# Gate and value weights loaded in pairs of row blocks, half of the low words cast on ScalarE, the scale of P in its cast, phi's sum on GpSimd

## The chip, the cores and the metric

The program runs on one core of a Trainium2 chip. The time is the device time of one execution in microseconds (us). The kernel before was timed three times; the median is 652.61 us (652.18 to 654.96). The profile was taken of one further execution of 654.12 us, whose traced span is 652.4 us.

Engines are called PE (TensorE, matmul), DVE (VectorE), ACT (ScalarE), POOL (GpSimd) and SP (the queue that issues nearly all DMAs). Each engine works through its own instructions in a fixed order, which is settled when the program is built.

## The reference, cut to what matters

```python
# attention: q, k, v of shape (4, 8, 576, 64)
a = softmax(causal(q @ k.T / sqrt(64)));  local = a @ v
phi(x) = where(x > 0, x, exp(x) - 1) + 1
mem = (phi(q) @ M_prev) / (phi(q) @ z_prev + 1e-6)
out = sigmoid(beta) * mem + (1 - sigmoid(beta)) * local
# gated FFN on x = out as (2304, 512)
xn = x / rms(x) * rms_g
y = (silu(xn @ w_gate) * (xn @ w_val)) @ w_out    # 512 -> 1536 -> 512
```

The weights w_gate, w_val (512 x 1536) and w_out (1536 x 512) arrive as float64 and are turned into float32 on the chip.

## The kernel before

**Tiling.** The 2304 rows are 18 blocks of 128 (n = 0 to 17), numbered so that blocks 0 and 1, 2 and 3 and so on form nine chunks (c = 0 to 8) of 256 rows for the FFN. A block's attention has a unit per head, or for short causal lengths per group of up to four heads.

**A unit of attention** (n from 2 on) goes through `u_scores` (matmuls of kT and qT in float16 high and low parts into `sc`; L514 or L538 on DVE adds the mask, writes S and the row minimum `nm`; L521 or L552 on DVE then adds the constant LNP = 15 ln 2 to `nm`), `u_exp` (L560 on ACT: exp(nm - S), so that P comes out times 2^15; L565 on ACT: cast to float16 P), `u_lo` (L574: the low half, S - P, on DVE, or for every second unit of blocks 4 to 7 on POOL; then one DMA transpose P to PT) and `u_pv` (L598 to L600: PT times v). Blocks 0 and 1 go through float32 forms of the same steps (`scores32`, `pv32`, `evac32`), which need no transposing DMA.

**phi** (`phi_calc`): exp on ACT (L355), then two instructions on DVE: min with 1 (L356), and max with q + 1 (L357). The result is cast, transposed by DMA to phT and multiplied with M (L635).

**The FFN** of chunk 0 runs in float32 (`m_proj`, L858: `gv` from xT and `wgv`; `m_down`, L912) since its weights are not yet split into float16 parts; chunks 1 to 8 run in float16 parts (L865 and L920 to L922). L858 needs both halves of xT of chunk 0, which blocks 0 and 1 write on DVE (L707), and all eight pieces of the first third of the weights.

**The weights.** w_gate and w_val are 24 pieces of 128 x 512 float64 (512 KB), ordered by third t, then gate or value, then row block cc. `load_w` (L744) brings a piece on SP's queue into one of six slots in the tile `wo`, which is not yet used for w_out; `w_conv` calls `f64_to_f32`, which runs ACT L774 (high word to float32), DVE L775 (low word shifted right by 29) and DVE L776 (the two joined), and then issues the load that takes the slot over. w_out follows in 12 pieces of the same size by `load_wo` and `wo_conv`, through the same function.

**What sets the order.** The work list `A` (attention) and lists of FFN closures are woven by `run` and `a_until` by hand-set targets; then the scheduler of the build places each instruction on its engine by its own simulated timeline and the priorities in `PRIO`. So an edit of durations or sizes can shift instructions anywhere.

Of the kernel before, what the change touches and what calls it, by code (L numbers as in the profile page):

```python
# [25 lines left out]
HORD = "k0 q0 M0 k1 q1 v0 M1 v1 w0 w1 w2 w3 w4 w5"  # L26
LAG = 3
LAG0 = 8
NA = 2
# [4 lines left out]
C1 = 8  # L34
# [10 lines left out]
P_HI = "a"  # L45
# [3 lines left out]
RING = 6  # L49
# [8 lines left out]
def attn_memory_moe_kernel(  # L58
# [435 lines left out]
    def u_scores(n, h0):  # L494
# [25 lines left out]

        nc.vector.tensor_scalar(nm0, nm0, LNP, None, op0=ALU.add)  # L521
        Ssb[(n, h0)] = (s, w, nm0)

    def tail_scores(n, h, s, nm, t, w):
# [27 lines left out]
        nc.vector.tensor_scalar(nm0, nm0, LNP, None, op0=ALU.add)  # L552
        Ssb[(n, h)] = (s, w + P, nm0)

    def u_exp(n, h0):
        s, w, nm = Ssb[(n, h0)]
        G = group(n)
        for g in range(G):
            v_ = s[:, g * w : (g + 1) * w]
            nc.scalar.activation(v_, v_, AF.Exp, bias=nm[:, g : g + 1], scale=-1.0)  # L560
        p16 = sb.tile([P, 2 * (NI * P + P)], F16, tag="P16", name="P16")
        if P_HI[(h0 // G) % len(P_HI)] == "d" and n < 4:
            nc.vector.tensor_copy(p16[:, : G * w], s[:, : G * w])
# [167 lines left out]
    NR = RING  # L731
    PRE = {"p": nc.gpsimd, "s": nc.sync, "a": nc.scalar}[PREQ]

    def hold(p, at):

        assert not any(abs(at - x) < 2 for x in held.values())
        held[p] = at
        return wo[:, at : at + 2, :].rearrange("p a f -> p (a f)")

    def load_w(m, cc, t):  # L740
        w = (w_gate, w_val)[m]
        p = piece(m, cc, t)
# [23 lines left out]
    def f64_to_f32(raw, dst, p):  # L766
# [5 lines left out]
        r = raw.rearrange("p (f w) -> p f w", w=2)  # L772
        ri, di = r.bitcast(I32), dst.bitcast(I32)
        nc.scalar.activation(dst, r[:, :, 1], AF.Prelu, scale=2.0 ** -112, alpha=2.0 ** 32)  # L774
        nc.vector.tensor_scalar(ri[:, :, 0], ri[:, :, 0], 29, None, op0=ALU.logical_shift_right)  # L775
        nc.vector.scalar_tensor_tensor(  # L776
            out=di, in0=di, scalar=3, in1=ri[:, :, 0], op0=ALU.logical_shift_left, op1=ALU.bitwise_or
# [252 lines left out]
    with tc.high_priority(HP) if HP else contextlib.nullcontext():  # L1030
# [3 lines left out]
            "M": load_M, "w": lambda p: load_w(*pcs[p]),  # L1034
# [150 lines left out]
    def conv(t):  # L1185
        return [lambda i=i: w_conv(i) for i, x in enumerate(pcs) if x[2] == t]
# [101 lines left out]
```

## Time and profile before

| what | value |
|---|---|
| three runs, median | 652.61 us |
| profiled execution | 654.12 us |
| its span | 652.4 us |
| outside the span | 1.7 us |
| PE busy | 607.4 us, 93% |
| DVE busy | 470.6 us, 72% |
| ACT busy | 384.5 us, 59% |
| POOL busy | 172.6 us, 26% |
| first float32 projection (L858) starts | 50.83 us |
| first down projection of chunk 0 (L912) starts | 124.24 us |

Busy time of PE is the union of matmuls whose ends are modelled, so a busy PE need not be at its peak. The profile's shares are means over stages: the first 50 us (loads, blocks 0 and 1), the stretch to about 145 us (chunk 0 of the FFN in float32, conversion of the weights, blocks 2 and 3), the stretch to about 240 us (weights split into float16 parts, blocks 4 to 7), and the rest, in which PE works almost without a gap. Idle time of an engine counts only where what it waits for is late.

### The profile page before, as it was taken

How to read it: one execution, taken by the hardware profiler on the slowest of the kernel's cores; microseconds unless marked ns; L12 is line 12 of the kernel's file. 1: busy time of each engine (PE TensorE's matmuls, PEld its weight loads, DVE VectorE, ACT ScalarE, POOL GpSimd, SP SyncE). 2: the span in 40 equal slices, each digit the busy share in tenths (PEclk: the TensorE clock that was granted, in tenths of full speed). 3: DMA queues.
4: the chain of work that ended last, by engine and by line, in shares of the span. 5: the costliest groups of instructions: out<-in, count | busy, mean ns of one | idle time of the engine just before them, and what ended most of it. 6: DMA issues, size and time to landing. Idle time of an engine off the chain costs nothing.

```text
span 652.4 us, 16021 instructions
## 1 busy us (share of the span) xinstructions
PE 607.4 (93%) x6131; PEld 473.9 (73%) x6131; DVE 470.6 (72%) x1444; ACT 384.5 (59%) x803; POOL 172.6 (26%) x257
## 2 busy tenths in 40 slices
PE   6789998797998789998999999999999999999996
PEld 4767787546866468787777787777878788888774
DVE  4787997877999666796877857967877757862221
ACT  3654675567689756575667666856665555442222
POOL 5020221210473333231242312522232212112211
PEclk8588998998999889999999999999999999999999
DMA  7995899529547897546759863595656464440001
GB/s 259 406 354 175 238 292 197 98 25 224 86 96 156 162 182 143 89 90 138 155 116 178 142 117 74 99 165 103 130 120 114 90 87 86 84 77 17 33 1 33
DMA packets 188524, 88.63 MB, mean 136 GB/s; under 512 B 173568, under 2 KB 173600, under 8 KB 188448
## 3 DMA queue, kind: packets, MB, share of 16 engines
q1 hardware_dynamic: 187680, 85.49, 60.3%
q0 software_dynamic: 768, 2.12, 1.0%
q8 instruction: 48, 0.79, 0.5%
q14 instruction: 28, 0.23, 0.1%
HBM read 36.20 MB, written 4.72 MB: 63 GB/s over the span
## 4 chain that ended last, share of the span: by engine, by line
PE 60%; DMA 14%; DVE 13%; ACT 7%; issue 3%; SPq 1%; POOL 0%; ACTq 0%; POOLq 0%; DVEq 0%
PE gv L865 29%; PE out L921 5%; PE out L920 5%; PE out L922 5%; PE out L912 3%; PE sc L508 3%; DMA phT<-row 3%; DMA PT<-P 2%; DMA wo<-in_moe_w_val_dram 2%; PE gv L858 2%; PE sc L534 2%; DMA kT<-row 2%; DVE S L514 2%; DVE P L574 2%; DMA kv<-in_qkv_dram 1%
## 5 line engine op out<-in xcount | busy, mean ns | idle before, releaser
L865 PE MATMUL gv<-xT,wgv 128*128 128x256 f16 x2304 | 313.9, 275 | 3.1 <-DMA xT<-x 3.1
L865 PEld LDWEIGHTS <-wgv 128*128 128x128 f16 x2304 | 221.9, 98 | 39.3 <-issue 4.2
L891 POOL TENSOR_TENSOR h<-th,h 128x256 f16<-128x256 f32 x96 | 73.1, 761 | 267.9 <-ACT h L890 210.0
L560 ACT ACTIVATE S<-S,nm 128x256 f32<-128x256 f32 (+4 forms) x128 | 75.5, 611 | 55.6 <-DVE nm L521 41.1
L508 PE MATMUL sc<-kT,qT 128*128 128x128 f16 x608 | 84.6, 222 | 3.5 <-DVE nm L514 1.5
L574 DVE TENSOR_TENSOR P<-S,P 128x512 f16<-128x512 f32 (+2 forms) x84 | 62.8, 748 | 34.4 <-ACT P L565 34.1
L876 DVE SCALAR_TENSOR_TENSOR th<-th,gv 128x256 f32<-128x256 f32 x96 | 39.9, 415 | 56.4 <-ACT th L875 55.9
L875 ACT ACTIVATE th<-gv,wt 128x256 f32<-128x256 f32 x96 | 44.9, 468 | 52.6 <-PE gv L865 51.6
L921 PE MATMUL out<-wo,h 128*128 128x512 f16 x192 | 72.8, 379 | 0.0
L920 PE MATMUL out<-wo,h 128*128 128x512 f16 x192 | 71.8, 379 | 0.0
L922 PE MATMUL out<-wo,h 128*128 128x512 f16 x192 | 71.6, 379 | 0.0
L514 DVE CUSTOM_DVE_ANT_0 S<-sc,mask,qsc 128x256 f32<-128x256 f32 (+3 forms) x112 | 62.1, 573 | 7.4 <-PE sc L508 5.5
L565 ACT CAST P<-S 128x512 f16<-128x512 f32 (+2 forms) x100 | 59.7, 597 | 10.0 <-DMA PT<-P 8.9
L890 ACT CAST h<-th 128x256 f16<-128x256 f32 x96 | 38.6, 402 | 43.8 <-DVE th L879 43.1
L598 PE MATMUL loc<-v,PT 128*128 128x65 f16 x304 | 50.6, 195 | 13.0 <-DMA PT<-P 12.8
L508 PEld LDWEIGHTS <-qT 128*128 128x128 f16 x608 | 51.4, 99 | 9.9 <-issue 3.1
L600 PE MATMUL loc<-v,PT 128*128 128x65 f16 x304 | 50.4, 195 | 0.0
L599 PE MATMUL loc<-v,PT 128*128 128x64 f16 x304 | 50.3, 195 | 0.0
L879 DVE SCALAR_TENSOR_TENSOR th<-th,wt,gv 128x256 f32<-128x256 f32 x96 | 45.8, 477 | 1.7
L858 PE MATMUL gv<-xT,wgv 128*128 128x256 f32 x192 | 46.8, 397 | 0.1
L598 PEld LDWEIGHTS <-PT 128*128 128x128 f16 x304 | 29.5, 98 | 19.4 <-DMA PT<-P 16.6
L858 PEld LDWEIGHTS gv<-xT,wgv 128*128 128x128 f32 x192 | 36.9, 198 | 6.2 <-issue 0.9
(226 smaller groups left out, 1112.9 us busy)
## 6 DMA issues: line engine op xcount, KB each, us to landing
kv<-in_qkv_dram SPq DMA_DIRECT2D x16, 512.0 KB, 4.5
wo<-in_moe_w_gate_dram SPq DMA_DIRECT2D x12, 512.0 KB, 7.8
wo<-in_moe_w_val_dram SPq DMA_DIRECT2D x12, 512.0 KB, 6.5
q<-in_qkv_dram SPq DMA_DIRECT2D x18, 256.0 KB, 3.1
wo<-in_moe_w_out_dram SPq DMA_DIRECT2D x8, 512.0 KB, 4.3
qT<-qT SPq DMA_DIRECT2D x32, 128.0 KB, 2.6
out_dram<-res SPq DMA_DIRECT2D x16, 256.0 KB, 2.4
pre<-in_qkv_dram POOLq DMA_DIRECT2D x8, 256.0 KB, 7.3
```

The costliest lines, as they stand in the source:

```text
L508: nc.tensor.matmul(t[:, g * w + j * P : g * w + (j + 1) * P], qT[n][:, t2, h, :], kT[blk_of[(b, j)]][:, h, :], start=(t2 == 0), stop=(t2 = ...
L514: nc.vector.tensor_tensor_reduce(out=s[:, g * w : (g + 1) * w], in0=t[:, g * w : (g + 1) * w], in1=mask[:, m0 : m0 + w], scale=qsc[n][:, 5:6],
L560: nc.scalar.activation(v_, v_, AF.Exp, bias=nm[:, g : g + 1], scale=-1.0)
L565: nc.scalar.copy(p16[:, : G * w], s[:, : G * w])
L574: eng.tensor_tensor(p16[:, w : 2 * w], s[:, :w], p16[:, :w], ALU.subtract)
L598: nc.tensor.matmul(a, phi_, vhi, start=(j == 0), stop=False)
L858: nc.tensor.matmul(o, wgv[:, 1 + p, o0 : o0 + P], xT[0][:, cc, :], start=(cc == 0), stop=(cc == NC - 1))
L865: nc.tensor.matmul(o, lhs, xT[c][:, rhs, :], start=(cnt == 0), stop=(cnt == 3 * NC - 1))
L891: nc.gpsimd.tensor_tensor(h16[:, 1], th, h16[:, 0], ALU.subtract)
L920: nc.tensor.matmul(o, hh, whi, start=(f == 0), stop=False)
L921: nc.tensor.matmul(o, hh, wlo, start=False, stop=False)
L922: nc.tensor.matmul(o, hl, whi, start=False, stop=(f == NF - 1))
```

## The change

Four edits.

1. `load_w(k)` brings two row blocks (1 MB) in one DMA into a slot of twice the size; three slots instead of six. There are 12 such loads instead of 24, and `w_conv(k)` converts 128 x 1024 at a time.
2. In `f64_to_f32` the low word of every second call (odd k of the pairs, odd f of w_out) is shifted by an ACT activation (Copy with a scale and a bias that truncates, written as an integer) instead of DVE's shift.
3. LNP is no longer added to `nm`, except in the units whose low half is on POOL. Instead the casts of P carry the factor 2^15: `hi_cast` (ACT, with a constant scale) and `lo_cast` (DVE scalar_tensor_tensor, S times the constant minus P).
4. For n >= 2 phi's q + 1 is computed in place on POOL (tensor_scalar), and one DVE instruction does min and max.

```diff
-HORD = "k0 q0 M0 k1 q1 v0 M1 v1 w0 w1 w2 w3 w4 w5"
+HORD = "k0 q0 M0 k1 q1 v0 M1 v1 w0 w1 w2"
-RING = 6
+RING = 3
         nc.scalar.activation(ph, qst[n], AF.Exp)
-        nc.vector.tensor_scalar(ph, ph, 1.0, None, op0=ALU.min)
-        nc.vector.scalar_tensor_tensor(
-            out=ph, in0=qst[n], scalar=1.0, in1=ph, op0=ALU.add, op1=ALU.max
-        )
+        if n < NA:
...
+        else:
+            nc.gpsimd.tensor_scalar(qst[n], qst[n], 1.0, None, op0=ALU.add)
+            nc.vector.scalar_tensor_tensor(
+                out=ph, in0=ph, scalar=1.0, in1=qst[n], op0=ALU.min, op1=ALU.max
+            )
@@ u_scores (tail_scores drops the line altogether)
-        nc.vector.tensor_scalar(nm0, nm0, LNP, None, op0=ALU.add)
+        if lo_on_pool(n, h0):
+            nc.vector.tensor_scalar(nm0, nm0, LNP, None, op0=ALU.add)
@@ u_exp, u_lo
-            nc.scalar.copy(p16[:, : G * w], s[:, : G * w])
+            hi_cast(p16[:, : G * w], s[:, : G * w], PSCALE)
-        eng = nc.gpsimd if lo_on_pool(n, h0) else nc.vector
-        eng.tensor_tensor(p16[:, w : 2 * w], s[:, :w], p16[:, :w], ALU.subtract)
+        if lo_on_pool(n, h0):
+            nc.gpsimd.tensor_tensor(p16[:, w : 2 * w], s[:, :w], p16[:, :w], ALU.subtract)
+        else:
+            lo_cast(p16[:, w : 2 * w], s[:, :w], PSCALE, p16[:, :w])
@@ load_w
-        raws[p] = hold(p, 2 * (p % NR))
+        m, cc, t = pcs[2 * k]
+        raws[k] = hold(k, 4 * (k % RING), 2)
         nc.sync.dma_start(
-            out=raws[p].bitcast(I64), in_=w[cc * P : (cc + 1) * P, t * 512 : (t + 1) * 512]
+            out=raws[k].bitcast(I64),
+            in_=(w_gate, w_val)[m][cc * P : (cc + 2) * P, t * 512 : (t + 1) * 512].rearrange(
+                "(a p) f -> p a f", a=2
+            ),
         )
@@ f64_to_f32
-        nc.vector.tensor_scalar(ri[:, :, 0], ri[:, :, 0], 29, None, op0=ALU.logical_shift_right)
+        if p % 2:
+            nc.scalar.activation(
+                top, low, AF.Copy, bias=-0.5 + 15.0 * 2.0 ** -21, scale=2.0 ** -29 - 2.0 ** -49
+            )
+        else:
+            nc.vector.tensor_scalar(top, words(raw.bitcast(I32))[..., 0], 29, None, op0=ALU.logical_shift_right)
@@ w_conv
-        f64_to_f32(raws.pop(p), wgv[:, 1 + p, :], i)
+        f64_to_f32(raws.pop(k), wgv[:, 1 + p : 3 + p, :], k)
```

The built order shifts with it. On DVE, where the scores of block 0 begin, the kernel before has the first weight piece (L775 and L776) between block 0's copies (L375) and the scores' masking (L429), interleaved with block 1's phi:

```order
L375 COPY q_0_148<-tp 128x512
L775 TENSOR_SCALAR wo<-wo 128x512
L356 TENSOR_SCALAR ph<-ph 128x512
L776 SCALAR_TENSOR_TENSOR wgv<-wgv,wo 128x512
L357 SCALAR_TENSOR_TENSOR ph<-q_120,ph 128x512
L429 ISA S,nm_163<-sc,mask 128x128
```

At the same place on DVE the changed kernel has (its lines L379, L355, L356 and L433 are the former L375, L356, L357 and L429):

```order
L379 COPY q_0_145<-tp 128x512
L355 TENSOR_SCALAR ph<-ph 128x512
L356 SCALAR_TENSOR_TENSOR ph<-q_120,ph 128x512
L433 ISA S,nm_160<-sc,mask 128x128
L433 ISA nm_160 128x1
```

No weight stands ahead of block 0's scores any more; the first conversion follows behind them. Down to the second write of xT (L707 before) DVE has 14 shifts and 13 joins of 128 x 512 before, and 3 shifts and 5 joins of 128 x 1024 now, beside one shift of w_out in both.

On DVE, in the units of block 2 (about 102 us in the trace of before), two heads are masked (L514, `nm` is the row minimum), and LNP's addition (L521) stands behind the low half of another unit, a join and an FFN step:

```order
L514 ISA nm 128x1
L574 TENSOR_TENSOR P_840<-S,P_840 128x512
L776 SCALAR_TENSOR_TENSOR wo<-wo,rawo_1550 128x512
L876 SCALAR_TENSOR_TENSOR h32v<-h32v,gv_1273 128x256
L521 TENSOR_SCALAR nm<-nm 128x2
L514 ISA S,nm<-sc,mask,qsc 128x256
```

In the changed kernel, on DVE at that place (L518 is the former L514, L792 the former L776):

```order
L895 SCALAR_TENSOR_TENSOR h32v<-h32v,gv_1217 128x256
L518 ISA S,nm<-sc,mask,qsc 128x256
L518 ISA nm 128x1
L518 ISA S,nm<-sc,mask,qsc 128x256
L518 ISA nm 128x1
L792 SCALAR_TENSOR_TENSOR wo<-wo,rawo_1453 128x512
```

`nm` is complete with the masking itself, and no instruction stands between it and ACT's exp.

On PE, the last float32 projection of chunk 0 (L858, gate and value of the last 128 columns) stands in the kernel before behind the first 24 products of PT and v of block 2, between scores and sums of squares of the weights (L146):

```order
L508 LDWEIGHTS qT_817
L508 MATMUL sc<-kT_857,qT_817 128x128
L858 MATMUL gv_1339<-xT_307,wgv 128x256 x8
L146 LDWEIGHTS wo
L146 MATMUL csum<-wo 128x128
```

In the changed kernel, on PE, it is complete (L874 is the former L858) ahead of the first such product (L603, the former L598):

```order
L874 MATMUL gv_1283<-xT_304,wgv 128x256 x5
L512 LDWEIGHTS qT_777
L512 MATMUL sc<-kT_726,qT_777 128x128
L874 MATMUL gv_1283<-xT_304,wgv 128x256 x3
L603 LDWEIGHTS PT
L603 MATMUL loc_0_859<-v_0_562,PT 128x65
```

The projections have moved ahead of the attention of blocks 2 and 3. From chunk 1 on the two orders of PE keep within a few units of each other.

## Rows read from the trace of the kernel before

**Rows 1.** The page, busy time (us), share of the span and instructions of each engine.

```profile
PE 607.4 (93%) x6131; PEld 473.9 (73%) x6131; DVE 470.6 (72%) x1444; ACT 384.5 (59%) x803; POOL 172.6 (26%) x257
```

**Rows 2.** Busy time by stretch, instructions in brackets; granted clock as share of full.

```profile
core 0: us, PE busy (x) PEld busy (x) DVE busy (x) ACT busy (x) POOL busy (x), PEclk, DMA share, GB/s
...
60.00:80.00 20.00, 19.94 (x127) 16.00 (x125) 18.88 (x66) 12.30 (x23) 4.79 (x5) 1.00 0.63 179
...
100.00:120.00 20.00, 15.18 (x161) 12.99 (x159) 15.35 (x54) 10.60 (x23) 3.63 (x4) 0.91 0.77 157
...
220.00:240.00 20.00, 13.64 (x172) 11.29 (x172) 13.73 (x43) 13.27 (x27) 5.72 (x8) 0.74 1.03 207
460.00:500.00 40.00, 40.00 (x426) 31.43 (x425) 31.09 (x97) 26.01 (x56) 10.85 (x16) 1.00 0.66 125
```

**Rows 3.** Who PE waited for over the span: us in total, times, longest.

```profile
PE loc L598 <- DMA PT<-P: 12.8, 13, 2.3
...
PE mem L635 <- DMA phT<-row: 4.0, 3, 3.3
PE gv L865 <- DMA xT<-x: 3.1, 1, 3.1
```

**Rows 4.** PE's timeline: first projection, first down projection (start, us, instruction, count).

```profile
50.83 6.41 PE L858 MATMUL gv<-xT,wgv 128*128 128x256 f32 x22
...
124.24 7.11 PE L912 MATMUL out<-wo,h32e 128*128 128x512 f32 x16
```

**Rows 5.** DVE's timeline at the start; in brackets the idle time before and its releaser.

```profile
13.43 0.43 DVE L775 TENSOR_SCALAR wo<-wo 128x512 int32<-128x512 int32 x1 [2.13 <-DMA wo<-in_moe_w_gate_dram]
...
15.37 0.28 DVE L429 CUSTOM_DVE_ANT_0 S<-sc,mask 128x128 f32<-128x128 f32 x1
...
17.40 0.69 DVE L375 COPY k<-tp 128x512 f32<-128x512 f32 x1
...
30.46 0.43 DVE L775 TENSOR_SCALAR wo<-wo 128x512 int32<-128x512 int32 x1 [1.06 <-DMA wo<-in_moe_w_val_dram]
```

**Rows 6.** Groups by line and shape: count, busy us, mean ns of one, idle before.

```profile
L774 ACT ACTIVATE wgv<-wo 128x512 f32<-128x512 f32 x24 | 15.3, 673 | 5.8 <-DMA wo<-in_moe_w_val_dram 3.0 <-DMA wo<-in_moe_w_gate_dram 2.8
...
L775 DVE TENSOR_SCALAR wo<-wo 128x512 int32<-128x512 int32 x32 | 13.5, 421 | 4.8 <-DMA wo<-in_moe_w_val_dram 2.2 <-DMA wo<-in_moe_w_gate_dram 2.1 <-DMA wo<-in_moe_w_out_dram 0.4
...
L776 DVE SCALAR_TENSOR_TENSOR wgv<-wgv,wo 128x512 int32<-128x512 int32 x24 | 16.4, 684 | 2.1 <-ACT wgv L774 1.6
...
L574 DVE TENSOR_TENSOR P<-S,P 128x384 f16<-128x384 f32 x24 | 15.3, 638 | 5.9 <-ACT P L565 5.9
...
L574 DVE TENSOR_TENSOR P<-S,P 128x640 f16<-128x640 f32 x16 | 14.3, 895 | 3.9 <-ACT P L565 3.8
...
L565 ACT CAST P<-S 128x512 f16<-128x512 f32 x52 | 31.9, 614 | 6.8 <-DMA PT<-P 6.3
...
L521 DVE TENSOR_SCALAR nm<-nm 128x1 f32<-128x1 f32 x64 | 9.5, 148 | 0.8
...
L356 DVE TENSOR_SCALAR ph<-ph 128x512 f32<-128x512 f32 x18 | 8.7, 484 | 6.4 <-ACT ph L355 5.8 <-POOL v L116 0.5
```

**Rows 7.** ACT's waits for `nm` from 50 to 250 us, then one unit's timeline.

```profile
ACT S L560 <- DVE nm L521: 10.4, 10, 3.2
...
112.41 0.09 DVE L514 DVE_READ_ACCUMULATOR2_ANT nm<- 128x1 f32 x1
...
114.01 0.17 DVE L521 TENSOR_SCALAR nm<-nm 128x2 f32<-128x2 f32 x1
...
114.22 0.92 ACT L560 ACTIVATE S<-S,nm 128x256 f32<-128x256 f32 x2 [2.65 <-DVE nm L521]
```

**Rows 8.** POOL's two shapes of 128 x 512, and one low half on DVE beside POOL's work.

```profile
L229 POOL COPY Mz<-M 128x512 f32<-128x512 f32 x2 | 1.2, 610 | 6.4 <-DMA M<-in_M_prev_dram 6.4
...
L116 POOL TENSOR_TENSOR v<-kv,v 128x512 f16<-128x512 f32 x18 | 22.6, 1269 | 41.2 <-ACT v L113 41.2
...
185.33 1.51 DVE L574 TENSOR_TENSOR P<-S,P 128x384 f16<-128x384 f32 x1
```

More of the change, by code (lines that the diff above doesn't have):

```diff
@@ L33 @@
 T32 = "dadda"
-C1 = 8
 C2 = 8
@@ L551, in tail_scores @@
         nm0 = nm[:, 1:2]
-        nc.vector.tensor_scalar(nm0, nm0, LNP, None, op0=ALU.add)
         Ssb[(n, h)] = (s, w + P, nm0)
@@ L561, in u_exp @@
         p16 = sb.tile([P, 2 * (NI * P + P)], F16, tag="P16", name="P16")
-        if P_HI[(h0 // G) % len(P_HI)] == "d" and n < 4:
-            nc.vector.tensor_copy(p16[:, : G * w], s[:, : G * w])
+        if lo_on_pool(n, h0):
+            nc.scalar.copy(p16[:, : G * w], s[:, : G * w])
         else:
-            nc.scalar.copy(p16[:, : G * w], s[:, : G * w])
+            hi_cast(p16[:, : G * w], s[:, : G * w], PSCALE)
         Ssb[(n, h0)] = (s, G * w, p16)
@@ L730, in attn_memory_moe_kernel, with hold, load_w @@
     raws = {}
-    NR = RING
     PRE = {"p": nc.gpsimd, "s": nc.sync, "a": nc.scalar}[PREQ]
[L734 to L742, printed above, removed]
-        raws[p] = hold(p, 2 * (p % NR))
+    def hold(p, at, n=1):
+        assert not any(at < y and x < at + 2 * n for x, y in held.values())
+        held[p] = (at, at + 2 * n)
+        r = wo[:, at : at + 2 * n, :].rearrange("p (a b) f -> p a (b f)", a=n)
+        return r if n > 1 else r[:, 0]
+    def load_w(k):
+        m, cc, t = pcs[2 * k]
+        raws[k] = hold(k, 4 * (k % RING), 2)
         nc.sync.dma_start(
-            out=raws[p].bitcast(I64), in_=w[cc * P : (cc + 1) * P, t * 512 : (t + 1) * 512]
+            out=raws[k].bitcast(I64),
+            in_=(w_gate, w_val)[m][cc * P : (cc + 2) * P, t * 512 : (t + 1) * 512].rearrange(
+                "(a p) f -> p a f", a=2
+            ),
         )
@@ L766, in f64_to_f32, with words @@
     def f64_to_f32(raw, dst, p):
-        r = raw.rearrange("p (f w) -> p f w", w=2)
-        ri, di = r.bitcast(I32), dst.bitcast(I32)
-        nc.scalar.activation(dst, r[:, :, 1], AF.Prelu, scale=2.0 ** -112, alpha=2.0 ** 32)
-        nc.vector.tensor_scalar(ri[:, :, 0], ri[:, :, 0], 29, None, op0=ALU.logical_shift_right)
+        def words(x):
+            return x.rearrange("p a (f w) -> p a f w" if len(x.shape) == 3 else "p (f w) -> p f w", w=2)
+        high, low = words(raw)[..., 1], words(raw.bitcast(U32))[..., 0]
+        top, di = words(raw.bitcast(I32))[..., 0], dst.bitcast(I32)
+        nc.scalar.activation(dst, high, AF.Prelu, scale=2.0 ** -112, alpha=2.0 ** 32)
+        if p % 2:
+            nc.scalar.activation(
+                top, low, AF.Copy, bias=-0.5 + 15.0 * 2.0 ** -21, scale=2.0 ** -29 - 2.0 ** -49
+            )
+        else:
+            nc.vector.tensor_scalar(top, words(raw.bitcast(I32))[..., 0], 29, None, op0=ALU.logical_shift_right)
         nc.vector.scalar_tensor_tensor(
-            out=di, in0=di, scalar=3, in1=ri[:, :, 0], op0=ALU.logical_shift_left, op1=ALU.bitwise_or
+            out=di, in0=di, scalar=3, in1=top, op0=ALU.logical_shift_left, op1=ALU.bitwise_or
         )
@@ L1033, in attn_memory_moe_kernel @@
             "q": load_q, "k": lambda n: load_half(n, 0), "v": lambda n: load_half(n, 1),
-            "M": load_M, "w": lambda p: load_w(*pcs[p]),
+            "M": load_M, "w": load_w,
         }
@@ L1113, in attn_memory_moe_kernel, with w_conv @@
                     a(n + 1, w, fn)
-    def w_conv(i):
-        m, cc, t = pcs[i]
-        p = piece(m, cc, t)
-        f64_to_f32(raws.pop(p), wgv[:, 1 + p, :], i)
-        held.pop(p)
-        if i + RING < len(pcs):
-            load_w(*pcs[i + RING])
+    def w_conv(k):
+        p = piece(*pcs[2 * k])
+        f64_to_f32(raws.pop(k), wgv[:, 1 + p : 3 + p, :], k)
+        held.pop(k)
+        if k + RING < len(pcs) // 2:
+            load_w(k + RING)
     def wo_conv(f):
@@ L1185, in conv @@
     def conv(t):
-        return [lambda i=i: w_conv(i) for i, x in enumerate(pcs) if x[2] == t]
+        return [lambda k=k: w_conv(k) for k in range(len(pcs) // 2) if pcs[2 * k][2] == t]
     def spl(t):
@@ L1196, in attn_memory_moe_kernel @@
     run(conv(0), cum[marks[1]] * HEADA)
-    run(conv(1)[:C1], cum[marks[1]])
+    run(conv(1), cum[marks[1]])
     a1, a3 = cum[marks[1]], cum[marks[3]]
-    run(zipped(conv(1)[C1:], projs(0, 4)), a1 + (a3 - a1) * A1)
+    run(projs(0, 4), a1 + (a3 - a1) * A1)
     run(zipped(conv(2), projs(4, 8)), a1 + (a3 - a1) * A2)
```

5 lines of the change are left out of this document (4 added, 1 removed).

## The prediction

> **What bounds the kernel now.** I read the page first: PE is busy for 93% of the span and DVE for 72% [rows 1]. The busy time by stretch says where these differ from what a change of DVE's work can reach. From about 240 us on PE has hardly a gap (40.00 of 40 us between 460 and 500), so work taken from DVE, ACT or POOL there buys next to nothing. Before that, PE stands at 15.18 of 20 us between 100 and 120 and at 13.64 between 220 and 240, with the granted clock at 0.91 and 0.74, so partly at the lower of its two levels, 1.2 GHz [rows 2]. PE's waits name the causes: transposed P (12.8 us in 13 waits), transposed phi (4.0), transposed x (3.1) [rows 3]. And the first projection of chunk 0 starts only at 50.83 us, the first down projection at 124.24 us [rows 4]. So the question is how much earlier PE's dense work can begin, and how much smaller the holes up to 240 us become. Whatever is won there should reach the end, since behind it PE runs a fixed amount of work without a gap.
>
> **The head, up to 50.83 us.** DVE is the engine that blocks 0 and 1 run on, and before the change it also waits for weights in order: 2.13 us at 13.43 for the first piece, 1.06 us at 30.46 for a value piece [rows 5]. The scores of block 0 start at 15.37 behind the first of these, and block 1's copy of k at 17.40. In the new order no weight stands ahead of the scores, so they can start some 2 us earlier; then comes the first pair, which needs 1 MB to be there. Work of DVE ahead of the second write of xT: before 14 shifts at 421 ns, 13 joins at 684 ns and a shift of w_out at 421, together 15.2 us [rows 6]. No row shows a join or shift of 1,024 columns. DVE's slope is (895 - 638) / 256 = 1.0 ns a column [rows 6], which makes a join 684 + 514, about 1,200 ns. The shift works faster per column: with the same fixed part, 638 - 384 x 1.0 = 252 ns, it is 252 + 2 x (421 - 252) = 590 ns; the ends are 421 and 842. Five joins, three shifts and the shift of w_out are then 5 x 1.20 + 3 x 0.59 + 0.42 = 8.2 us. So 7.0 us leave the path's engine, beside up to 3.2 us of waits. Not all of it was on the path: DVE also waits for PE and ACT there, and ACT's blocks of 1,024 columns delay the squares that x needs by up to one block (673 ns to twice that [rows 6]). I take 5 us, bounds 0 and 8. What stood behind those weights is late next: PE's own float32 work of block 1, and the clock, which may still be low when the projections start early.
>
> **The stretch from 50 to 125 us.** Here DVE is full (18.88 of 20 us between 60 and 80) and so is PE (19.94) [rows 2]: both must get shorter or start earlier together. All 36 conversions cost DVE 36 x (0.421 + 0.684) = 39.8 us before and 6 x 0.59 + 6 x 0.42 + 12 x 1.20 + 12 x 0.684 = 28.6 us now: 11 us less, 7 of them counted above, the other 4 here. More weighs the chain of each unit. At 112.41 the row minimum is read; LNP's addition starts at 114.01, behind a low half and a join of weights, and ACT's exp at 114.22, after 2.65 us of idling. ACT waits for that addition 10 times in 50 to 250 us, 10.4 us together [rows 7]. With the addition gone the exp can start at 112.5, 1.7 us earlier. The eight units of blocks 2 and 3 go one behind another through DVE, ACT and the transposing DMA, and PE waits for them: the 4.8 us that it is idle between 100 and 120 [rows 2] are what can be won. PE's order helps less than before, since the last projection, 16 matmuls, no longer fills a gap between the units. I take 3 us, bounds 0 and 5.
>
> **Later.** 84 of 100 additions go, 84 x 0.148 = 12.4 us of DVE, and 16 of phi's min at 0.484, 7.7 us [rows 6]. Up to 240 us the transposing DMAs set the pace (share 1.03 between 220 and 240 [rows 2]), beyond that PE does. I take 1.5 us, bounds 0 and 4. The new forms of P's two casts cost nothing that I can see: an activation with a constant scale takes 673 ns on strided words against 614 for the cast, and a join with a constant 684 against 638 to 895 for a subtraction of 384 to 640 columns [rows 6]. Were ACT's cover (59% busy) gone, 84 x 0.06 = 5 us of ACT would show.
>
> **What it adds.** ACT gets 6 casts of 128 x 512 at 673 ns and 6 of twice that size (0.67 to 1.35), 8 to 12 us, of which about half fall where ACT is 12.30 of 20 us busy; hidden. POOL gets 16 sums of 128 x 512. No row shows one; a POOL copy of that shape takes 610 ns, a sum of two tensors 1,269 [rows 8]. I take 0.7, near the copy, since it too reads one tensor. Each lies in phi's way in place of a min of 0.484, so phi is later by 0.1 to 0.8 us, plus POOL's queue ahead of it (splits of v at 1,269), and behind phi wait DVE's next instruction, the cast, SP's transpose to phT and PE's 4.0 us of waits for it [rows 3]. And DVE can be slower beside POOL: one low half took 1.51 us [rows 8] against 0.638 in the mean [rows 6]. I take 2 us for all this, bounds 0 and 8. The 12 loads fewer are SP issues that are hidden.
>
> **The sum.** 654.1 us (profiled execution: span 652.4 and 1.7 outside) - 5 - 3 - 1.5 + 2 = 646.6 us. That execution lies 1.5 us above the median of the runs, so the prediction is **645.1 us**. The likeliest case's own range, with the ends of its terms not all at once, is 639 to 650.
>
> **Rivals.**
>
> *The gain is given back before 240 us (chance 0.22).* From 200 to 240 us PE waits on transposing DMAs, whose engines are full [rows 2]. For: what feeds them there is the splitting of the weights and blocks 4 to 7, little touched by the change. Against: their inputs too come from engines that are ahead by then. If all but the later term is lost, 654.1 - 1.5 + 1 - 1.5 = 652; with a quarter of the 8 us kept, 650. Call it 651.
>
> *PE starves between 100 and 125 us and its clock falls (0.08).* The projections stand ahead of all units now. If PE is through with them before the units come, the hole grows by the two 8-matmul halves, some 4 us at the rate of 22 in 6.41 us [rows 4], and the clock, which went down to 0.74 in the stretch where PE was idle for 6.4 of 20 us [rows 2], falls during chunk 0's down projection. Half a stretch of 20 us at half the clock loses 5 us. That is 4 + 5 - 3 = 6 above the median, 658.6. It decides if the last PT of block 3 lands later than 124 us.
>
> *POOL's sums hold DVE (0.07).* If each of the 16 costs DVE what the slow low half shows, 1.51 - 0.64 = 0.87 us, and all were on the path, 14 us come on top of a gain of 9.5: 652.6 + 14 - 9.5 = 657. It decides once more than ten of the sixteen overlap work of DVE that PE waits for. The Trainium skill, page "SBUF — State Buffer", section "Who interferes with whom", gives a rule behind that row: a VectorE instruction that reads two SBUF tensors and a GpSimd one that reads SBUF exclude each other for their whole length. By that rule the sums would cost up to their own length each, and the time would be the 657 of this rival; that POOL is only 26% busy speaks against it.
>
> **How the numbers follow.** Forecast 0.63, given back 0.22, starving 0.08, POOL 0.07. Within 0.5% (649.3 to 655.9 us) is about what a measurement of this kernel can tell from no change. The forecast's own spread puts little of it above 649.3, and a few of the "given back" cases end below: faster 0.62, same 0.24, slower 0.14. The range is 638.5 (head and units at their better bounds) to 655 (nothing kept, some of the additions paid), which leaves out most of the two slower rivals and the luckiest cases.
>
> **What would show it.** In the profile after: the first projection starts at 43 to 47 us; the first down projection of chunk 0 at 114 to 119 us; no wait of exp on an addition outside blocks 4 to 7; PE's idle time between 100 and 125 us below 5 us; DVE busy near 445 us. Wrong if the first projection comes at 50 us, if DVE waits at the first pair of 1 MB for more than 2 us, if phT waits exceed 8 us, or if the clock is at its lower level in a stretch where it was not before.

## The result, and the profile after

The changed kernel takes 659.44 us (median of five runs, 658.51 to 660.76), the kernel before 653.75 us (five runs, 652.18 to 655.30). The ratio is 1.0089, with a 95% interval of 1.0061 to 1.0116: it is 5.8 us slower, where 645.1 us and faster were forecast. Its profiled execution has a span of 658.8 us. Executions more than 1.5% above the fastest of the same kernel are left out of every ratio in this document: two in the first experiment, one in the fourth, two in the fifteenth.

The page of the changed kernel, busy time (us), share of the span and instructions of each engine, against [rows 1]:

```profile
PE 609.2 (92%) x6131; PEld 473.5 (72%) x6131; DVE 450.8 (68%) x1308; ACT 391.3 (59%) x803; POOL 193.6 (29%) x273
```

DVE did lose 20 us (to 450.8, where the forecast had near 445). PE didn't lose any, and the span grew by 6.4. Where PE's dense work begins, from PE's timeline (start, us, instruction, count; in brackets the idle time before), against [rows 4]:

```profile
43.19 3.72 PE L874 MATMUL gv<-xT,wgv 128*128 128x256 f32 x16
...
121.73 7.13 PE L928 MATMUL out<-wo,h32e 128*128 128x512 f32 x16 [0.33 <-DVE wmx L811]
...
143.67 1.58 PE L881 MATMUL gv<-xT,wgv 128*128 128x256 f16 x13
```

The first projection comes 7.6 us earlier, the first down projection only 2.5 us. Not all of the 7.6 belongs to the change. DVE's second write of xT, for which the projection waits, starts 4.9 us earlier (the changed kernel, then before):

```profile
42.14 0.69 DVE L712 TENSOR_TENSOR xT<-xtp,rg 128x512 f32<-128x512 f32 x1 [0.43 <-PE xtp L709]
```

```profile
47.01 0.69 DVE L707 TENSOR_TENSOR xT<-xtp,rg 128x512 f32<-128x512 f32 x1 [0.45 <-PE xtp L704]
```

The rest lies on PE, whose granted clock between 40 and 60 us was 0.74 in the trace of before and 1.00 in this one. In another trace with the old order up to there (the eighteenth experiment's, below) the first projection starts at 48.01 us and the first down projection at 120.05. Against that trace the changed kernel is 4.8 us ahead at the one and 1.7 us behind at the other. So of the head's gain 2.5 us at most are left at the first down projection.

Chunk 1's first projection, which started at 146.14 before, keeps the 2.5 us; the other 9 us are lost behind it. Where, PE's own count tells: of the 2,304 float16 matmuls of L865 (L881 now) each chunk has 288, so the first, the 289th and so on start a chunk (us):

| first projection of | before | changed | difference |
|---|---|---|---|
| chunk 1 | 146.14 | 143.67 | -2.5 |
| chunk 2 | 231.43 | 230.53 | -0.9 |
| chunk 3 | 296.61 | 300.55 | +3.9 |
| chunk 4 | 359.74 | 366.59 | +6.9 |
| chunk 5 | 419.68 | 426.15 | +6.5 |
| end of the span | 652.39 | 658.77 | +6.4 |

So 1.6 us are lost in chunk 1, 7.8 between 231 and 367 us, and nothing behind that. Busy time by stretch (columns as in [rows 2]), first of the changed kernel:

```profile
100.00:120.00 20.00, 13.06 (x153) 10.90 (x153) 16.44 (x54) 12.91 (x29) 5.52 (x6) 0.77 0.83 185
...
160.00:180.00 20.00, 17.51 (x188) 14.81 (x187) 16.13 (x63) 11.10 (x23) 6.58 (x7) 0.91 0.49 73
...
260.00:280.00 20.00, 17.80 (x210) 13.93 (x208) 12.61 (x35) 10.68 (x23) 5.29 (x7) 1.00 0.70 125
```

and of the kernel before, for the two stretches that [rows 2] doesn't have:

```profile
160.00:180.00 20.00, 19.50 (x215) 16.70 (x214) 18.50 (x70) 12.99 (x27) 7.78 (x8) 1.00 0.60 101
...
260.00:280.00 20.00, 19.04 (x232) 15.21 (x229) 14.60 (x44) 12.75 (x27) 6.18 (x8) 1.00 0.52 84
```

Between 100 and 120 us PE works 2.1 us less than before, and its granted clock, partly at the lower level already, falls from 0.91 to 0.77. Between 160 and 180 it is 0.91 where it was 1.00, but between 140 and 160 it is 1.00 where it was 0.91; over the span it is 0.960 against 0.962, so the clock explains little of the loss. The later holes are small, 1.2 to 2.0 us more in 20 than before, and there are several. Who PE waited for (us in total, times, longest), against [rows 3]:

```profile
PE loc L603 <- DMA PT<-P: 12.3, 15, 2.5
...
PE sc L512 <- DMA qT<-qT: 3.7, 3, 2.0
PE sc L512 <- DVE nm L518: 2.7, 1, 2.7
PE sc L512 <- DMA kT<-row: 2.6, 2, 2.4
```

The waits for phT and for xT, 4.0 and 3.1 us before, are nearly gone. In their place PE waits for the transposed q and k and for the row minimum, thus for the scores to begin. Between 50 and 125 us, two of these waits stand at 84.86 and 107.14:

```profile
84.86 0.27 PE L512 MATMUL sc<-kT,qT 128*128 128x128 f16 x2 [1.96 <-DMA qT<-qT]
...
107.14 1.35 PE L512 MATMUL sc<-kT,qT 128*128 128x128 f16 x12 [2.37 <-DMA kT<-row]
```

The prices of the new forms, by line and shape (count | busy us, mean ns of one):

```profile
L360 POOL TENSOR_SCALAR q<-q 128x512 f32<-128x512 f32 x16 | 25.7, 1608 | 24.7 <-DVE row L95 12.5 <-ACT ph L353 6.3 <-DVE pw L122 5.9
...
L792 DVE SCALAR_TENSOR_TENSOR wgv<-wgv,wo 128x1024 int32<-128x1024 int32 x12 | 14.6, 1220 | 0.5 <-ACT wo L787 0.5
...
L787 ACT ACTIVATE wo<-wo 128x1024 int32<-128x1024 uint32 x6 | 6.8, 1126 | 0.0
...
L791 DVE TENSOR_SCALAR wo<-wo 128x1024 int32<-128x1024 int32 x6 | 4.1, 691 | 2.5 <-DMA wo<-in_moe_w_val_dram 2.5
```

The join (1,220 ns, estimated 1,200) is as the prediction had it; ACT's shift (1,126) and DVE's (691, estimated 590) lie within its bounds. POOL's sum takes 1.5 to 2.0 us where 0.7 was taken.

### The profile page after: what moved, and what is told of

Same layout as the page of the kernel before. It is cut to its first block, busy times and chain, and to the rows that moved or that the text cites. A ratio compares the mean times of both kernels' runs of the same rounds, so it can differ in the third digit from the quotient of the medians.

```text
span 658.8 us, 15865 instructions
## 1 busy us (share of the span) xinstructions
PE 609.2 (92%) x6131; PEld 473.5 (72%) x6131; DVE 450.8 (68%) x1308; ACT 391.3 (59%) x803; POOL 193.6 (29%) x273
## 4 chain that ended last, share of the span: by engine, by line
PE 58%; DMA 15%; DVE 12%; ACT 7%; issue 5%; SPq 1%; POOL 1%; ACTq 0%; DVEq 0%; POOLq 0%
PE gv L881 28%; DMA PT<-P 5%; PE out L937 4%; PE out L936 4%; PE out L938 4%; PE sc L512 3%; PE gv L874 3%; DMA kv<-in_qkv_dram 3%; DMA wo<-in_moe_w_val_dram 2%; DMA wo<-in_moe_w_out_dram 2%; ACT junk L241 2%; DVE P L95 2%; DVE S L518 1%; PE sc L538 1%; PE out L928 1%
## 5 line engine op out<-in xcount | busy, mean ns | idle before, releaser
L881 PE MATMUL gv<-xT,wgv 128*128 128x256 f16 x2304 | 315.2, 275 | 2.8 <-DVE th L895 2.3
L881 PEld LDWEIGHTS <-wgv 128*128 128x128 f16 x2304 | 222.0, 98 | 40.3 <-issue 4.6
L95 DVE SCALAR_TENSOR_TENSOR P<-S,P 128x512 f16<-128x512 f32 (+2 forms) x84 | 61.0, 726 | 31.7 <-ACT P L92 30.9
L518 DVE CUSTOM_DVE_ANT_0 S<-sc,mask,qsc 128x256 f32<-128x256 f32 (+3 forms) x112 | 61.8, 573 | 19.1 <-PE sc L512 16.8
L603 PE MATMUL loc<-v,PT 128*128 128x65 f16 x304 | 50.6, 196 | 12.4 <-DMA PT<-P 12.3
L92 ACT ACTIVATE P<-S 128x512 f16<-128x512 f32 (+2 forms) x84 | 51.7, 615 | 8.9 <-DMA PT<-P 7.7
L874 PE MATMUL gv<-xT,wgv 128*128 128x256 f32 x192 | 45.7, 386 | 0.1
L603 PEld LDWEIGHTS <-PT 128*128 128x128 f16 x304 | 29.7, 99 | 19.8 <-DMA PT<-P 16.2
L678 POOL TENSOR_TENSOR t<-t,t 128x256 f32<-128x256 f32 x32 | 24.9, 778 | 56.8 <-DVE t L674 41.2
```

The lines of the kernel that those rows point to most:

```text
L92: nc.scalar.activation(dst, src, AF.Copy, scale=scale)
L95: nc.vector.scalar_tensor_tensor(out=dst, in0=src, scalar=scale, in1=hi, op0=ALU.mult, op1=ALU.subtract)
L518: nc.vector.tensor_tensor_reduce(out=s[:, g * w : (g + 1) * w], in0=t[:, g * w : (g + 1) * w], in1=mask[:, m0 : m0 + w], scale=qsc[n][:, 5:6],
L603: nc.tensor.matmul(a, phi_, vhi, start=(j == 0), stop=False)
L874: nc.tensor.matmul(o, wgv[:, 1 + p, o0 : o0 + P], xT[0][:, cc, :], start=(cc == 0), stop=(cc == NC - 1))
L881: nc.tensor.matmul(o, lhs, xT[c][:, rhs, :], start=(cnt == 0), stop=(cnt == 3 * NC - 1))
```

## The experiments

All ratios are against the kernel before on the same chip, with 95% intervals; "us" is the ratio less 1, times 653.6 us. The kernel before spread by 7 to 10 us on each chip. Up to chunk 2, two traces with the same instructions in the same order (before and the eighteenth) stand 5.9 us apart, so a difference of this size there between two single traces is not one between kernels.

### One edit alone, and one edit undone

Experiments 1 to 4 take the hunks of one edit of the diff into the kernel before; the build then makes its own order. Experiments 5 to 8 leave the hunks of one edit out of the changed kernel. For edit 2, for instance:

```diff
-        if p % 2:
+        if False:
             nc.scalar.activation(top, low, AF.Copy, ...)
```

The first experiment, edit 4 alone:

> The kernel before with edit 4 alone: phi's q + 1 on POOL for n >= 2, one DVE instruction for min and max. Theory P (POOL's sum makes the loss: each of the 16 takes 1.5 us in the trace after, not the 0.7 that the prediction took, and phi, its transpose and q's buffer come later): 4 to 8 us slower than the kernel before, and the changed kernel without edit 4 is then about as much faster than it. Theory S (the loss comes from the weights' edits, which put the projections ahead of the attention of blocks 2 and 3): within 2 us of the kernel before. The prediction's own term was +2 us.

The second, edit 3 alone:

> The kernel before with edit 3 alone: no addition of LNP to the row minimum except where the low half is on POOL; the factor 2^15 in P's two casts. The prediction's term: 3 to 4.5 us faster (84 additions of 0.148 us go, the exp starts earlier, DVE near 458 us busy). Rival C (the casts with a factor cost more than the additions, or the new order eats what they give): no faster than the kernel before, 0 to 4 us slower. Theories P and S: this edit is innocent, so some us faster.

The third, edit 1 alone:

> The kernel before with edit 1 alone: gate and value weights loaded and converted two row blocks at a time (three slots of 1 MB), both low words shifted on DVE, LNP and phi as before. Theory S: the first projection starts near 44 us instead of 50.8, but the first down projection comes at 121 us or later, since PE waits between 84 and 121 us for the units of blocks 2 and 3, and the whole is 0 to 4 us slower. The prediction's term (the head's gain kept): 4 to 6 us faster, first down projection at 118 us.

The fourth, edit 2 alone:

> The kernel before with edit 2 alone, in pieces of 128 x 512: the low word of every second piece of the weights shifted by an ACT activation instead of DVE (18 of 36). The prediction's reading: ACT's 18 x 0.67 us = 12 us are hidden, DVE gives up 18 x 0.42 = 7.6 us, so 0 to 2 us faster. Rival A (ACT is crowded between 80 and 110 us and its casts of x, q and P come later): 1 to 4 us slower, with the first down projection later than 124.2 us.

The fifth to eighth, the changed kernel without edit 4, without 3, without 1 and without 2:

> The changed kernel without edit 4 (phi's min and max both on DVE again). Theory P (POOL's sums of 1.5 us make the loss): 5 to 9 us faster than the changed kernel, 648 to 653 us. Theory O (a single edit's price is small, and the order that the build makes of them decides): anywhere within 6 us of the changed kernel, and not what edit 4 alone did to the kernel before (+1.6 us) with the sign turned.

> The changed kernel without edit 3 (LNP added to the row minimum everywhere, plain casts of P). Alone on the kernel before, edit 3 cost 13.5 us. If it costs the same here (its casts or its missing additions are dear in themselves), this kernel takes some 646 us, faster than both. Theory O (edit 3 alone was dear through the order of the build, which another starting point changes): less than 7 us is won, 652 us or more.

> The changed kernel without edit 1 (weights in single pieces of 512 KB, every second low word on ACT). Alone on the kernel before, edit 1 cost 3.9 us. Theory S (pairs lose what the head wins): 2 to 6 us faster than the changed kernel, with the first projection back at 50 us. The prediction's term: 4 to 6 us slower.

> The changed kernel without edit 2 (all low words on DVE, in pairs of row blocks). Alone on the kernel before, edit 2 cost 3.5 us in the timed runs though its profiled run was as long as that of before. Theory A (ACT crowded): 2 to 4 us faster than the changed kernel. The prediction: 0 to 3 us slower.

| edit | alone, ratio | us | changed kernel without it, ratio | us |
|---|---|---|---|---|
| 1 (pairs) | 1.0059 (1.0025 to 1.0092) | +3.9 | 1.0144 (1.0103 to 1.0185) | +9.4 |
| 2 (ACT's shift) | 1.0053 (1.0024 to 1.0082) | +3.5 | 1.0168 (1.0133 to 1.0202) | +11.0 |
| 3 (scale in the casts) | 1.0206 (1.0164 to 1.0248) | +13.5 | 1.0058 (1.0034 to 1.0081) | +3.8 |
| 4 (sum on POOL) | 1.0025 (0.9989 to 1.0060) | +1.6 | 1.0076 (1.0042 to 1.0109) | +5.0 |
| all | 1.0089 (1.0061 to 1.0116) | +5.8 | | |

No single edit explains it. The theory of this stage that POOL's sum makes the loss falls in both tests, by the totals: alone it costs 1.6 us, and taking it out gives back 0.8. The theory on the pairs has the sign right alone (+3.9) and wrong undone: without them the changed kernel is slower still. What was expected of the head held only in part: the first projection starts at 47.05 us in the third experiment (near 44 expected) and at 47.45 in the seventh (50), and in the fourth the first down projection comes early, at 118.87, though the kernel is slower. And edit 3, which takes work from DVE and adds none, is the dearest alone. Its trace shows what such a loss looks like. PE's longest wait there, at the first projection of chunk 1:

```profile
153.62 5.78 PE L866 MATMUL gv<-xT,wgv 128*128 128x256 f16 x27 [7.63 <-DMA xT<-x]
```

Before this was one wait of 3.1 us [rows 3]. Nothing in edit 3 makes the transpose of x longer; the build has put work ahead of it. The last products of PT and v of block 3, from which x is computed, begin on PE behind 42 of the 48 matmuls of chunk 0's down projection, and behind 20 in the kernel before (first this kernel, then before):

```profile
142.43 0.19 PE L599 MATMUL loc<-v,PT 128*128 128x65 f16 x1
```

```profile
133.31 0.20 PE L598 MATMUL loc<-v,PT 128*128 128x65 f16 x1
```

So the transpose of x goes out at 150.51 us instead of 140.60.

### The same edits in the order of the kernel before

So the edits were run again with every engine's instructions held to the order of the kernel before. This adds an ordering edge between neighbours on an engine, without a wait; instructions that the kernel before doesn't have are placed freely.

```diff
+    for row in order_of_the_kernel_before:       # one row for each engine
+        for last, i in zip(row, row[1:]):
+            tc.add_manual_dep(i, last.name, no_sync)
```

PE's row is then that of the kernel before, instruction by instruction. The kernel before was not itself run with its order held, so what holding does by itself was not measured. The ninth experiment, edit 3:

> Edit 3 alone (as in the second experiment, which took 13.5 us longer than the kernel before), but with every engine's instructions held to the order of the kernel before: an ordering edge between neighbours on an engine, without any wait; only the 84 additions are missing from DVE's row. Theory O (the edits are cheap, the order that the build makes of them is what costs): 1 to 5 us faster than the kernel before, as the prediction's term of 3 us had it. Theory D (the casts with a factor are dear in themselves): again 8 us or more slower.

It takes 0.9956 (0.9933 to 0.9979), 2.9 us less than the kernel before, and 16 us less than the same instructions in the build's order. Theory O holds for it. The wait for xT is back at 3.2 us.

The tenth, edit 4; its sum waits for q's split, so phi on DVE had to be free as well:

> Edit 4 alone, in the order of the kernel before; POOL's sums and phi's one instruction on DVE are placed freely, since the sum overwrites q and has to wait until q's own split has read it. Theory O: within 2 us of the kernel before. Theory D: POOL's sum of 1.5 us and its wait for q's split are paid at each of the 16 blocks, 3 to 8 us slower, and PE waits for phT.

1.0171 (1.0130 to 1.0211), 11.2 us slower: here theory D holds. Where it is paid, in one block, in order of time over the engines:

```profile
291.07 0.75 DVE L97 SCALAR_TENSOR_TENSOR row<-q,qsc,row 128x512 f16<-128x512 f32 x1
...
291.91 1.50 POOL L362 TENSOR_SCALAR q<-q 128x512 f32<-128x512 f32 x1 [3.26 <-DVE row L97]
...
293.45 0.69 DVE L363 SCALAR_TENSOR_TENSOR ph<-ph,q 128x512 f32<-128x512 f32 x1 [1.62 <-POOL q L362]
...
294.17 0.72 ACT L94 ACTIVATE row<-ph,qsc 128x512 f16<-128x512 f32 x1 [3.64 <-DVE ph L363]
...
294.93 0.75 DVE L97 SCALAR_TENSOR_TENSOR row<-ph,qsc,row 128x512 f16<-128x512 f32 x1 [0.79 <-ACT row L94]
...
295.71 0.41 DVE L553 CUSTOM_DVE_ANT_0 S<-sct,tmask,nm 128x128 f32<-128x128 f32 x1
...
296.18 0.61 PE L540 MATMUL sc<-kT,qT 128*128 128x128 f16 x8 [2.30 <-DVE nm L553]
```

The sum overwrites q, so it waits for the low half of q's split. DVE stands 1.62 us for POOL, ACT 3.64 us for phi, then DVE for ACT, and the mask that PE waits for is queued behind: PE stands 2.30 us. Over the span ACT waits for phi 9.1 us in five places, where it didn't wait for it at all before.

The eleventh, edits 1 and 2:

> Edits 1 and 2 together (the weights in pairs, every second low word on ACT), in the order of the kernel before; the new loads and conversions are placed freely. Theory O: the first projection near 44 us and the first down projection near 119 us, 3 to 6 us faster than the kernel before. Theory D: the first down projection at 121 us or later and no gain at the end.

0.9948 (0.9924 to 0.9972), 3.4 us faster. Its first down projection:

```profile
119.22 7.11 PE L922 MATMUL out<-wo,h32e 128*128 128x512 f32 x16
```

That is 5.0 us earlier than in [rows 4], but the edits are not shown to be the cause: with the same row of PE it comes at 119.73 us in the ninth experiment's trace, without edits 1 and 2, and at 120.05 in the eighteenth's, without any edit. And the first projection, expected near 44 us, starts at 48.97. DVE's second write of xT, here and in the eighteenth:

```profile
46.31 0.69 DVE L706 TENSOR_TENSOR xT<-xtp,rg 128x512 f32<-128x512 f32 x1 [0.17 <-PE xtp L703]
```

```profile
46.51 0.67 DVE L707 TENSOR_TENSOR xT<-xtp,rg 128x512 f32<-128x512 f32 x1
```

So in the old order edits 1 and 2 don't bring the head's gain. Theory O is right on the total alone, and where the 3.4 us are won the traces don't show. The twelfth, all four edits:

> All four edits, so the work of the changed kernel, in the order of the kernel before (what is new is placed freely). Theory O: the sum of the prediction's terms, 644 to 649 us by a kernel before of 653 us, so 9 us or more faster than the changed kernel with the same instructions. Theory D: no faster than the kernel before.

1.0083 (1.0048 to 1.0119), 5.4 us slower: no better than the changed kernel, and not the 9 us better that theory O asked for. By the tenth experiment edit 4 is the reason. So, thirteenth, edits 1 to 3 without it:

> Edits 1, 2 and 3 without edit 4, in the order of the kernel before. If the gains of the ninth and eleventh experiments add up and edit 4 alone is what was dear in that order: 0.990 of the kernel before, 647 to 649 us, faster than both kernels; the same instructions in the order that the build makes of them took 658.6 us (fifth experiment). If the gains don't add: 650 to 652 us.

0.9963 (0.9936 to 0.9991), 650.84 us: faster than both kernels, by 2.4 us than the one before. The order is worth 7 us here: the fifth experiment has the same instructions at +5.0. Between the twelfth and this one lie 7.8 us, the price of edit 4 on top of the others. But the gains, 2.9 and 3.4 us, don't add. Why is open.

### Whether a new order loses by itself

The fourteenth is the reverse, the old work in the order of the changed kernel (conversions and phi placed freely):

> The reverse: the work of the kernel before (all additions, mins, single pieces of weights), in the order of the changed kernel; what the changed kernel doesn't have is placed freely, phi on DVE too. Theory O (the order itself is worse): 656 us or more, 3 to 9 us slower than the kernel before. If the order is innocent: within 2 us of the kernel before.

1.0506 (1.0478 to 1.0535): 33 us. An order may fit only the work that it was made for; this says more about a row of instructions that meets other durations than about the new order with its own work. The same caution holds for the order of the kernel before: what an edit costs when held to it is its price in an order made without it. So, as the eighteenth, the kernel before was built with one priority changed by 1%, which moves its instructions (PE's row differs from 235 us on):

```diff
-PRIO = (500, 600, 100, 900)
+PRIO = (500, 600, 101, 900)
```

> The kernel before with one number of the build's priorities changed, 100 to 101 (units from block 4 on): the same instructions in another order from some 200 us on. Theory O (the order of the kernel before is a good one among many, and any edit that lets the build order anew loses it): 2 to 10 us slower than the kernel before. If the order weighs little: within 2 us of it.

0.9978 (0.9950 to 1.0006): no loss. That any new order loses is wrong, at least behind 235 us. And -1.4 us (-3.3 to +0.4) without any edit is not far from the gains of 2.4 to 3.4 us above. What the runs show is a draw: with the same instructions, edit 3 differs by 16 us between two orders, edits 1 to 3 by 7, edit 4 by 10 in the other direction, and the unchanged work by 33 us in the changed kernel's order and not at all here.

That edit 4 comes out cheap in the build's order (+1.6 alone, 0.8 on top of the others) doesn't make the sum free there. From the first projection of chunk 2 to the end, all nine traces with the sum on POOL (the changed kernel and experiments 1, 6, 7, 8, 10, 12, 16 and 17) take 425.3 to 430.9 us, in whatever order. Of the eleven without it nine take 420.7 to 423.7; the other two are the second experiment (428) and the fourteenth (440). The changed kernel takes 428.2, the kernel before 421.0. The fifth experiment, the changed kernel without the sum, takes 421.8 there and loses ahead of it: its chunk 2 starts at 235.27 us, the changed kernel's at 230.53. So the two tie in total, but not by the same loss.

### Why the sum on POOL is dear

Three kernels in the order of the kernel before. The fifteenth, with the sum on DVE, still over q:

```diff
-            nc.gpsimd.tensor_scalar(qst[n], qst[n], 1.0, None, op0=ALU.add)
+            nc.vector.tensor_scalar(qst[n], qst[n], 1.0, None, op0=ALU.add)
```

> As the tenth experiment (edit 4 in the order of the kernel before, 11 us slower), but with phi's in-place sum on DVE instead of POOL: it still overwrites q and waits until q's split has read it, but takes some 0.5 us and needs no other engine. Theory W (the wait for q's split makes the loss: phi can no longer be computed before q is split): again 6 us or more slower than the kernel before. Theory L (POOL's length of 1.5 us and its queue make it): at most 3 us slower.

1.0056 (1.0028 to 1.0083), 3.7 us, between the two theories: what is left without POOL, the wait for q's split among it, costs about a third of the 11.2. The sixteenth, with the sum on POOL in a tile of its own:

```diff
-            nc.gpsimd.tensor_scalar(qst[n], qst[n], 1.0, None, op0=ALU.add)
+            q1 = sb.tile([P, HD], F16, tag="junk", name="q1", bufs=1)
+            nc.gpsimd.tensor_scalar(q1, qst[n], 1.0, None, op0=ALU.add)
```

> As the tenth experiment, but POOL's sum goes to a tile of its own instead of over q (in float16, in the space that ACT's squares write to without a reader, so phi is rounded and the squares wait for its reader): it needn't wait for q's split any more, and still takes some 1.5 us. Theory W: at most 3 us slower than the kernel before. Theory L: 6 us or more slower.

1.0213 (1.0185 to 1.0242), but ACT's squares, which share that space, waited 13.3 us for phi. The edit brought in a wait of its own, so it doesn't tell. In the seventeenth phi stays on DVE as before, and the sum on POOL comes behind it, read by nobody:

```diff
             out=ph, in0=qst[n], scalar=1.0, in1=ph, op0=ALU.add, op1=ALU.max
         )
+        if n >= NA:
+            nc.gpsimd.tensor_scalar(qst[n], qst[n], 1.0, None, op0=ALU.add)
```

> The kernel before in its own order, phi computed on DVE as before; in addition POOL adds 1 to q in place, 16 times, behind phi, and nobody reads it. So POOL has the tenth experiment's load (16 x 1.5 us) and DVE has POOL beside it, but phi waits for neither. Theory L1 (POOL's load by itself, in its queue or beside DVE, makes the 11 us): 5 us or more slower than the kernel before. Theory L2 (it is phi's chain through POOL that costs: q's split, sum, phi, ACT's cast, one behind another): within 2 us of the kernel before.

1.0129 (1.0082 to 1.0175), 8.4 us, with phi's chain untouched. So theory L2 falls as the whole story. Who waits then is SP, whose loads of q (L234) and M (L227) need q's slot (us, times, longest), in this kernel:

```profile
SPq L234 <- POOL q L361: 17.5, 9, 5.1
...
SPq L227 <- POOL q L361: 3.6, 2, 2.3
```

and in the kernel before, where phi's last instruction frees the slot:

```profile
SPq L234 <- DVE ph L357: 4.6, 3, 3.5
...
SPq L227 <- DVE ph L357: 0.6, 1, 0.6
```

SP issues one behind another, so the transposes of x, k and P stand behind the load. SP's timeline at one such place, first with the sum (POOL's sum runs from 250.48 to 251.98 us), then before:

```profile
252.01 1.14 SPq L227 DMA_DIRECT2D M<-in_M_prev_dram  x2
253.25 1.26 SPq L723 DMA_TRANSPOSE xT<-x  x1
```

```profile
249.96 1.14 SPq L227 DMA_DIRECT2D M<-in_M_prev_dram  x2
251.25 1.23 SPq L721 DMA_TRANSPOSE xT<-x  x1
```

The transpose goes out 2.0 us later, though its input was ready only 0.4 us later, and ACT's next cast then stood 4.57 us for it instead of 2.83 (with the sum, then before):

```profile
258.23 0.72 ACT L94 ACTIVATE row<-ph,qsc 128x512 f16<-128x512 f32 x1 [4.57 <-DMA xT<-x]
```

```profile
256.07 0.72 ACT L94 ACTIVATE row<-ph,qsc 128x512 f16<-128x512 f32 x1 [2.83 <-DMA xT<-x]
```

In the tenth experiment the same loads wait for phi: L234 8.1 us in five places, L227 3.8. The fifteenth experiment takes POOL away and leaves 3.7 us, the seventeenth takes phi's chain away and leaves 8.4. How the 8 to 11 us divide between the late slot, phi's chain and POOL's load by itself is open.

What POOL takes from DVE directly is small. DVE and POOL in the seventeenth experiment, around the sums at 250.48 and 471.35 us:

```profile
250.91 0.74 DVE L97 SCALAR_TENSOR_TENSOR x<-t,xs,x 128x512 f16<-128x512 f32 x1
251.58 0.14 DVE L523 TENSOR_SCALAR nm<-nm 128x1 f32<-128x1 f32 x1
251.64 0.73 DVE L97 SCALAR_TENSOR_TENSOR row<-kv,tcb,row 128x512 f16<-128x512 f32 x1
...
471.35 1.51 POOL L361 TENSOR_SCALAR q<-q 128x512 f32<-128x512 f32 x1
...
471.53 0.98 DVE L97 SCALAR_TENSOR_TENSOR x<-t,xs,x 128x512 f16<-128x512 f32 x1
...
472.43 0.45 DVE L523 TENSOR_SCALAR nm<-nm 128x2 f32<-128x2 f32 x1
472.50 0.38 DVE L124 TENSOR_SCALAR pw<-pw 128x2 int32<-128x2 int32 x1
```

Beside the first sum nothing is longer than before; at the second, three instructions are, by 0.22 to 0.29 us each. Matched one by one with the kernel before, the 84 DVE instructions that overlap a sum are 1.5 us longer in all (longer and shorter ones set off against each other). The Trainium skill, page "SBUF — State Buffer", section "Who interferes with whom", would have the two instructions of L97 at 250.91 and 251.64, which read two SBUF tensors, shut out for the length of the sum; by the spans of the trace they run inside it in 0.74 and 0.73 us, as long as in the kernel before (0.74 each), so the measurement decides against it here.

## Why the prediction was wrong, point by point

**The step that failed is the sum itself.** It added the prices of instructions as if they were put into one and the same order, and took the new order to be as good as the old, since from chunk 1 on "the two orders of PE keep within a few units of each other". As built, edits 1 to 3 cost 5.0 us instead of giving 9.5. And in one and the same order the sum fails too, on two terms: the gains (-9.5, measured -2.4) and what the change adds (+2, measured 7.8 on top of the other edits and 11.2 alone). The terms with the order held:

| term | predicted | with the old order held |
|---|---|---|
| edits 1 and 2 (head, and part of the stretch behind) | -5 and more | -3.4 (-5.0 to -1.8) |
| edit 3 (units, later) | -3 and more | -2.9 (-4.4 to -1.4) |
| edits 1 to 3 together | -9.5 | -2.4 (-4.2 to -0.6) |
| what it adds | +2 | +11.2 (8.5 to 13.8) for edit 4 alone |
| all | -7.5 | +5.4 (3.1 to 7.8) |

The range's lower end doesn't follow from the terms either: with head and units at their better bounds they give 640.1 us, not 638.5.

**The head.** Right in mechanism and in size as built: DVE's second write of xT comes 4.9 us earlier where 5 were forecast. The first projection's 7.6 us hold some 2.8 that belong to the trace of before. That the gain would reach the end was wrong: at most 2.5 us of it were left at the first down projection, as PE waited for q and k of the units that now stand behind the projections. This is in part the rival in which PE starves and its clock falls: PE was idle 6.9 us between 100 and 120, at 0.77, and 7.3 between 100 and 125, where less than 5 were to show it right. But the clock was at 0.98 between 120 and 140, in chunk 0's down projection, where that rival had it fall, and 9 us were lost behind this stretch; that the rival's 658.6 us lie near the measured time is chance. The rival "given back before 240 us" fits up to chunk 2, where 0.9 us are left, but had no loss behind it. Of the signs of being wrong, one came up nearly: DVE waited 2.5 us for a pair of value weights, though not for the first pair. And the gain hangs on the new order: in the old one edits 1 and 2 don't bring it.

**The units.** The exp no longer waits for an addition outside blocks 4 to 7. Between 50 and 250 us ACT's wait for the row minimum falls from 10.4 us [rows 7] to the following (beside 0.9 us for an addition that is left):

```profile
ACT S L563 <- DVE nm L518: 3.9, 3, 2.0
```

The edit is worth its 3 us where the order is held. Alone in the build's order it cost 13.5.

**"Later" and the gapless end.** PE does run without a gap from 440 us on. But the prediction let the gain pass through all that lies behind 240 us unharmed, because PE was nearly full there. It was nearly full in the old order with the old work; the changed kernel lost 7.8 us between 231 and 367, in small holes, and all nine traces with the sum on POOL are long in the stretch from chunk 2 on.

**What it adds.** The mis-sized term: 2 us with a bound of 8, measured at 11.2 in the old order (7.8 on top of the other edits). The sum's price was taken near a copy (610 ns); it is 1.5 us, more than the sum of two tensors in [rows 8]. And two things weren't counted: that a sum over q has to wait for q's split, and that q's slot comes free later, on which SP's loads wait with all transposes behind them. The rival on POOL had the right place and the wrong path: DVE is hardly held. "POOL is only 26% busy" was no argument, since the instruction stands in a chain and holds a slot.

**What is shown and what is not.** The changed kernel as built is slower, and undoing one edit doesn't mend it: without edit 4 it is at +5.0, without edit 3 at +3.8, without edit 1 or 2 slower still. It is shown that edits 1 to 3 lose 7 us by the build's order (fifth and thirteenth experiment), and that the sum on POOL costs 8 to 11 us in the old order; that it also makes the changed kernel's loss behind chunk 2 is read from where the traces are long, not from a run that changes it alone. Why the build's order for edits 1 to 3 is worse, and why the gains don't add, was not found.

## What to carry to other kernels

Where a build orders the instructions anew, measure an edit twice: as built, and with the old order held; the first tells what you ship, the second what the edit is worth in that order. Compare the two stretch by stretch: equal totals can hide different losses. Before moving an elementwise step to an idle engine, ask which buffer it overwrites or holds longer, and who loads into that buffer from an in-order queue. An engine's busy share says nothing of an instruction that stands in a chain.

## What was not expected of the hardware

- POOL's addition of a constant, 128 x 512 in float32, takes 1.48 to 2.30 us over all traces (mostly 1.50), longer than its sum of two tensors with a float16 result (1,269 ns) and 2.5 times its copy (610 ns) [rows 8].
- Two executions with the same row of PE instructions up to 235 us can differ by 4.2 us at the first down projection and by 5.9 us at chunk 2: the 22 matmuls of the first projection took 6.41 us in [rows 4], and in the eighteenth experiment's trace:

```profile
48.01 5.02 PE L858 MATMUL gv<-xT,wgv 128*128 128x256 f32 x22
```

The granted clock from 40 to 60 us was 0.74 in the one and 1.00 in the other. So a few us at the head of a single trace belong to neither kernel.
